# A spectral layer with two MLPs: x on all partitions, first transforms in four array tiles

## The chip, the cores and the metric

The kernel runs on one core of a Trainium2 chip. The metric is the time of one execution in device microseconds (us). The kernel before took 1102.35 us, the median of three runs (1100.9 to 1102.99).

## The reference, cut to what matters

```python
X = np.fft.rfft(x, axis=1)               # x: 2 x 3008 x 256, float32
Yr = Xr @ w_r - Xi @ w_i + b_r
Yi = Xr @ w_i + Xi @ w_r + b_i
Y = soft_threshold(Yr, 0.01) + 1j * soft_threshold(Yi, 0.01)
y = np.fft.irfft(Y, n=3008, axis=1)
h = y.reshape(6016, 256) @ w_in;   g = max(h, 0) + alpha * min(h, 0);    z = g @ w_out     # 2048 wide
h = z @ w_in2;   g = where(h >= 1, h, where(h <= -1, 0, (h + 1)**2 / 4));   out = g @ w_out2
```

All is computed in float32; products of the MLPs and of the mixing are made in three parts each from a high and a low half.

## The kernel before, in words

The transform of length 3008 is split as 47 x 64. A first transform of length 47 is a matmul with a constant (`c47`), for 24 frequencies k, cosine and sine. Its result `a` goes to memory (`a_dr`) and comes back with the 64 other positions in the partitions. A second transform per k (`psf`, from `a` and the constants `m`), the mixing with the weights (`psk`, `ri`), the threshold and the first half of the way back (`psi`, constants `n`) follow; its result `ve` goes through memory (`v_dr`) too, and `p3` (line 613) ends the way back. Then the two MLPs run.

x comes in 16 groups (two batches b, eight each; the host pads 47 rows to 48), each [96 partitions, 4, 256], 384 KB: two parities of position times 48 rows. `f1(g)` makes the first transform of group g in two PSUM banks, each with two matmuls of 256 columns (line 397); a float32 matmul appears in the profile as two records. ScalarE evicts one bank (line 399), VectorE the other (line 401), to `ae`. `store_a(g, h)` (line 375) writes half h of `ae` (48 partitions, 12 frequencies, 192 KB) to `a_dr[b][h]`, in pieces of 1 KB. `load_a(b, parts)` (line 371) reads some k of `a` back into `a_sb[b]`, [128 partitions, 24, 256].

Every engine works in the order in which the program is written; a planner sets nothing. SyncE (SP) issues nearly all transfers, in order, and waits before an issue whose inputs aren't ready; what stands behind waits too. Its order before is: the first eight groups of x; for each of the groups 0 to 7 its first store and the load of group g + 8; `load_a(0)` of k 0 to 3, then of 4 to 11, with constants between; the eight second stores of batch 0; constants; `load_a(0)` of k 12 to 23; constants; the first weights (line 147); the first stores of batch 1 and later, in the item loop, its second stores. ScalarE's queue issues `c47`, `alpha`, the bias and the two weight matrices `wm32`.

TensorE does the 16 first transforms, then 24 items (b, i), two k each, 12 a batch. In the loop over j, `psf` of item j + 2 (line 448, eight records) comes first, then `psk` of item j + 1, `ri` of item j and `psi` of item j - 2. At j = 2 and from j = 5 on, steps of the generator `conversions` are taken: they load MLP weights and split them on ScalarE, VectorE and GpSimd (POOL). The loads of `a` of batch 1 are issued at j = 5, 6 and 9.

Of the kernel before, what the change touches and what calls it, by code (L numbers as in the profile page):

```python
# [25 lines left out]
W_MAX = 122876.0 * 2.0 ** -16  # L26
NP = 6
CHUNKS = [512, 512, 512, 512, 512, 448]
PAIRS = [(0, 512), (1024, 512), (2048, 480)]


def fourier_constants():

    import numpy as np

    n1, k1 = np.arange(R1), np.arange(NK)
    a = 2 * np.pi * (np.outer(n1, k1) % R1) / R1

    c = np.zeros((2, 48, 2, 2, NK))
    for par in range(2):  # L40
        c[par, :R1, 0, par] = np.cos(a)
        c[par, :R1, 1, par] = -np.sin(a)
    c = c.reshape(96, 4, 2, NK // 2).transpose(0, 2, 1, 3).reshape(96, 96)

    g = np.zeros((2, 64, 64))
    g[:, 0:96 // 2:2, :R1] = np.cos(a).T
    g[:, 1:96 // 2:2, :R1] = -np.sin(a).T
    g = g.reshape(128, 64)

    t, par, k2 = np.arange(NT), np.arange(2), np.arange(R2)  # L50
    n2 = t[:, None] + 32 * par[None, :]
    m = np.zeros((NT, 2, 2, NK, 2, R2))
    w = np.zeros((2, R2, NK, 2, 2, NT))
    for k in range(NK):
        freq = k + R1 * k2
# [39 lines left out]
def spectral_mlp_kernel(ctx: ExitStack, tc: tile.TileContext, x, w_r, w_i, bias, c_f1, c_f2,  # L95
                        c_i1, c_i2, w_in1, w_out1, alpha, w_in2, w_out2, out):
    nc = tc.nc
    V, A, G, T = nc.vector, nc.scalar, nc.gpsimd, nc.tensor
# [3 lines left out]
    psum = ctx.enter_context(tc.tile_pool(name="psum", bufs=2, space=PSUM))  # L102
    dram = ctx.enter_context(tc.tile_pool(name="dram", bufs=1, space=DRAM))

    def split(src, hi, lo, hi_engine):

        if hi_engine is A:
            A.activation(hi, src, AF.Copy)  # L108
        else:
            V.tensor_copy(hi, src)  # L110
        V.tensor_tensor(lo, src, hi.bitcast(F32), op=ALU.subtract)  # L111
# [10 lines left out]
    def block(tag, shape, dtype, name):  # L122
        return base.tile(shape, dtype, tag=tag, name=name)
# [6 lines left out]
        p = block(f"p{npiece[0] % NP}", [128, 1024], F32R, name)  # L130
        return p[:, 112:112 + 768]

    a_dr = [[dram.tile([NT, 48, D], F32, name=f"a_dr{b}_{h}") for h in range(2)] for b in range(B)]
    v_dr = [dram.tile([96, NT, D], F32, name=f"v_dr{b}") for b in range(B)]


# [199 lines left out]
    def obank(shape, name, ahead=None):  # L336
# [2 lines left out]
        turn[0] += ahead is None  # L339
        return psum.tile(shape, F32, tag=f"o{k}", bufs=1, name=name)  # L340

    warm = rot.tile([128, 512], F32, tag="ta", name="warm")
    V.memset(warm, 0.0)
    ri = [psum.tile([128, 2, D], F32, tag=f"o{k}", bufs=1, name=f"ri{k}") for k in range(2)]
    for k in range(2):
        T.matmul(ri[k].rearrange("p z e -> p (z e)"), warm[:, 0:128], warm, start=True, stop=True)


    c47 = block("u2", [128, 1024], F32, "c47")[0:96, 0:96]
    A.dma_start(c47, c_f1)  # L350
    xs = {}

    def load_x(g):
        b, j = divmod(g, 8)
        tag = f"p{g}" if g < 6 else f"w{g - 6}" if g < 14 else f"c{g - 12}"
        xs[g] = block(tag, [96, 4, D], F32, f"x{b}_{j}")
        if g == 0:
            nc.sync.dma_start(xs[g][:, 0:1, :], x[b, j, :, 0:1, :])
            nc.sync.dma_start(xs[g][:, 1:4, :], x[b, j, :, 1:4, :])
        else:  # L360
            nc.sync.dma_start(xs[g], x[b, j])

    A_PARTS = ((0, 2), (2, 2), (4, 2), (6, 2), (8, 4), (12, 6), (18, 6))

    def load_a(b, parts):
        if a_sb[b] is None:
            a_sb[b] = block(f"a{b}", [128, NK, D], F32, f"a_{b}")
        for k, n in parts:
            h, k0 = divmod(k, NK // 2)
            src = a_dr[b][h].rearrange("t (q k) f -> (t q) k f", q=4)  # L370
            nc.sync.dma_start(a_sb[b][:, k:k + n, :], src[:, k0:k0 + n, :])

    def store_a(g, h):
        b, j = divmod(g, 8)
        nc.sync.dma_start(a_dr[b][h][4 * j:4 * j + 4].rearrange("t p f -> p t f"), aes[g][48 * h:48 * h + 48])

    def load_mn(k, tiles, src, h=None):

        s = slice(0, 8) if h is None else slice(4 * h, 4 * h + 4)
        nc.sync.dma_start(tiles[k][:, s, :].rearrange("p k f -> p (k f)"),  # L380
                          src[:, 1024 * k + 128 * s.start:1024 * k + 128 * s.stop])
# [2 lines left out]

    def f1(g):
        b, j = divmod(g, 8)
        if g < 10:
            ae = block(f"w{8 + g}" if g < 5 else f"m{1 + g}" if g < 8 else f"w{g - 8}", [96, 4, D], F32, f"ae{g}")
        else:
            if g == 10:  # L390
                late.append(block("a1", [96, 6, 4, D], F32, "ae_late"))
            ae = late[0][:, g - 10]
        aes[g] = ae
        for i in range(2):
            ps = psum.tile([96, 2, D], F32, tag="h" if i else "e", name=f"ps1_{b}_{j}_{i}")
            for u in range(2):
                T.matmul(ps[:, u, :], c47, xs[g][:, 2 * i + u, :], start=True, stop=True)
            if i == 0:
                A.activation(ae[:, 0:2, :], ps, AF.Copy)
            else:  # L400
                V.tensor_copy(ae[:, 2:4, :], ps)

    late = []
    for g in range(8):
        load_x(g)
# [9 lines left out]
    A.dma_start(b_t[0:1], bias)  # L415
    ones = rot.tile([1, 128], F32, tag="cm", name="ones")
    V.memset(ones, 1.0)
    for g in range(8):
        f1(g)
        store_a(g, 0)  # L420
        load_x(8 + g)
        if g == 3:
            load_mn(0, m_t, c_f2, 0)
        if g in (1, 2):
            A.dma_start(wm32[g - 1], (w_r, w_i)[g - 1].rearrange("(c p) e -> p c e", p=128))
    load_a(0, A_PARTS[:2])
    load_mn(0, m_t, c_f2, 1)
    load_a(0, A_PARTS[2:5])
    load_mn(1, m_t, c_f2, 0)
    load_mn(0, n_t, c_i1, 0)  # L430
    for g in range(8):
        store_a(g, 1)
    load_mn(1, m_t, c_f2, 1)
    load_mn(0, n_t, c_i1, 1)
    load_a(0, A_PARTS[5:])
    load_mn(1, n_t, c_i1)
    load_mn(2, m_t, c_f2)
    conv = conversions(0, list(range(NF)))
    next(conv)
    items = [(b, i) for b in range(B) for i in range(NK // 2)]  # L440
    xt, y_32, ve = {}, {}, {}

# [46 lines left out]
    wm = [block(t, [128, 2, 2, D], F32R, f"wm{k}") for k, t in enumerate(("c0", "c1", "w2"))]  # L489
    ws = [rot.tile([128, 2, D], F32, tag=t, name=f"ws{t}") for t in ("cm", "cp")]  # L490

    def split_wm(k, w):
        hi, lo = (wm[k][:, z].rearrange("p c (h q) -> p c q h", h=2) for z in range(2))
        split(w.rearrange("p c (q h) -> p c q h", h=2), hi, lo, A)

    for g in range(8, 16):
        f1(g)
        if g < 15:
            store_a(g, 0)
        if g == 8:  # L500
            T.matmul(ri[0].rearrange("p z e -> p (z e)"), ones, b_t[0:1].rearrange("p z e -> p (z e)"), start=True, stop=True)
            V.tensor_copy(b_t, ri[0])
        if g == 9:
            split_wm(0, wm32[0])
            V.scalar_tensor_tensor(ws[0], wm32[0], -1.0, wm32[1], op0=ALU.mult, op1=ALU.subtract)
        if g == 11:
            split_wm(1, ws[0])
            V.tensor_tensor(ws[1], wm32[1], wm32[0], op=ALU.subtract)
        if g == 13:
# [150 lines left out]
    n = len(items)  # L660
# [19 lines left out]
            ops[int(what[0])](what[1])  # L680
    for name in "HshLl":
        ops[2](name)
    store_a(15, 0)
    for j in range(n):
        parts = f2_parts(*items[j + 2]) if 0 < j < n - 2 else None
        if j + 1 < n:
# [4 lines left out]
        if j >= 2:  # L691
            i1(*items[j - 2])

        if j == 3:
            for g in range(8, 16):
                store_a(g, 1)
        if j == 5:
            load_a(1, A_PARTS[:2])
        if j == 6:
            load_mn(2, n_t, c_i1, 0)  # L700
            load_a(1, A_PARTS[2:3])
            load_mn(2, n_t, c_i1, 1)
            load_a(1, A_PARTS[3:5])
# [384 lines left out]
```

## Time and profile before

| what | value |
|---|---|
| median of three runs | 1102.35 us |
| profiled execution, its own time | 1102.65 us |
| its span | 1100.6 us |
| TensorE busy | 1087.2 us |
| VectorE busy | 897.4 us |
| ScalarE busy | 815.9 us |
| GpSimd busy | 36.9 us |
| moved by DMA | 101.19 MB |

The span runs from the first to the last instruction; the execution's own time has 2.05 us around it. A busy TensorE is not TensorE at its peak, since matmuls are pipelined and their ends are modelled: where it matters, starts are counted. L397 is line 397 of the kernel; PE is TensorE, PEld its weight loads, DVE VectorE, ACT ScalarE, POOL GpSimd, SP SyncE; a q behind the engine means its queue, which waits and issues transfers.

### The profile page before, as it was taken

Reading aid. Unit: us, or ns where it says so; the run is one execution under the profiler, and the core shown is the slowest. Engines: PE = TensorE matmul, PEld = TensorE weight load, DVE = VectorE, ACT = ScalarE, POOL = GpSimd, SP = SyncE. Lnnn points to the kernel's source line nnn. Section 1 sums busy time; section 2 is a strip of 40 time slices with the busy share of each in tenths; the row PEclk is TensorE's granted clock in tenths of the full one; section 3 lists DMA queues with packets and bytes.
Section 4 is the critical chain, followed back from the end, with each engine's and each line's share of the span. In section 5 each row is a group of like instructions: output and inputs, shape, how many; then the busy total and the mean of one; then the engine's idle time right before and its main releaser. Section 6 shows DMA issues by size and latency. Waiting matters only on the chain.

```text
span 1100.6 us, 17043 instructions
## 1 busy us (share of the span) xinstructions
PE 1087.2 (99%) x6368; PEld 955.7 (87%) x6368; DVE 897.4 (82%) x1572; ACT 815.9 (74%) x1499; POOL 36.9 (3%) x36
## 2 busy tenths in 40 slices
PE   9989999999999999999999999999999999999998
PEld 6878888888888998888889988888899888888897
DVE  3769759888879979989999877877878878878876
ACT  3557776656776768888888777877778878777876
POOL 0025400000000000000000000000000000000000
PEclk9999999999999999999999999999999999999999
DMA  9898754101322403324226720010010000100101
GB/s 265 299 277 261 204 142 108 39 1 67 126 97 97 171 20 115 115 96 141 89 97 248 273 90 1 1 39 1 1 38 1 37 1 1 39 1 1 39 1 37
DMA packets 49860, 101.19 MB, mean 92 GB/s; under 512 B 5009, under 2 KB 27249, under 8 KB 49778
## 3 DMA queue, kind: packets, MB, share of 16 engines
q1 hardware_dynamic: 48832, 99.41, 27.6%
q8 instruction: 50, 0.82, 0.3%
q10 hardware_dynamic: 946, 0.69, 0.2%
q14 instruction: 32, 0.26, 0.1%
HBM read 64.57 MB, written 35.52 MB: 91 GB/s over the span
## 4 chain that ended last, share of the span: by engine, by line
PE 82%; ACT 3%; DVE 2%; issue 0%; ACTq 0%; DVEq 0%
PE pq L114 10%; PE pq L115 10%; PE pq L116 10%; PE seeded L114 4%; PE seeded L116 4%; PE seeded L115 4%; PE psh L114 4%; PE pso L114 4%; PE psh L116 4%; PE psh L115 4%; PE pso L116 4%; PE pso L115 4%; PE psA L114 3%; PE psA L116 3%; PE psA L115 3%; PE psC L116 3%
## 5 line engine op out<-in xcount | busy, mean ns | idle before, releaser
L114 PE MATMUL pq<-gh,w 128*128 128x512 f32 (+1 forms) x576 | 216.6, 376 | 1.0 <-ACT yt L874 1.0
L115 PE MATMUL pq<-gl,w 128*128 128x512 f32 (+1 forms) x576 | 216.0, 375 | 0.4 <-DVE gl L845 0.2
L116 PE MATMUL pq<-gh,w 128*128 128x512 f32 (+1 forms) x576 | 215.8, 375 | 0.0
L842 ACT ACTIVATE gh<-ta 128x512 fp32r<-128x512 f32 (+1 forms) x144 | 88.0, 619 | 92.1 <-DVE ta L839 85.9
L641 ACT ACTIVATE ta<-psh,slopes 128x512 f32<-128x512 f32 (+1 forms) x96 | 65.1, 678 | 78.7 <-DVE ta L643 42.3
L114 PEld LDWEIGHTS pq<-gh,w 128*128 128x128 f32 x576 | 108.8, 189 | 15.9 <-ACT yt L874 3.1
L115 PEld LDWEIGHTS pq<-gl,w 128*128 128x128 f32 x576 | 108.9, 189 | 13.7 <-DVE gl L845 1.0
L116 PEld LDWEIGHTS pq<-gh,w 128*128 128x128 f32 x576 | 108.9, 189 | 12.8
L845 DVE TENSOR_TENSOR gl<-tb,gh 128x512 fp32r<-128x512 f32 (+1 forms) x96 | 65.3, 680 | 60.8 <-ACT gh L842 60.7
L845 DVE TENSOR_TENSOR gl<-ta,gh 128x512 fp32r<-128x512 f32 (+1 forms) x144 | 97.3, 676 | 3.1 <-ACT gh L842 1.4
L111 DVE TENSOR_TENSOR gl<-ta,gh 128x512 fp32r<-128x512 f32 (+1 forms) x96 | 65.2, 679 | 37.9 <-ACT gh L108 37.5
L933 DVE TENSOR_TENSOR h<-psC,s 128x512 f32<-128x512 f32 (+1 forms) x72 | 48.8, 678 | 40.8 <-PE psC L116 34.1
L114 PE MATMUL psh<-mxh,w 128*128 128x512 f32 (+1 forms) x192 | 72.2, 376 | 0.1
L114 PE MATMUL pso<-gh,w 128*128 128x512 f32 (+1 forms) x192 | 72.3, 377 | 0.0
L116 PE MATMUL pso<-gh,w 128*128 128x512 f32 (+1 forms) x192 | 71.9, 375 | 0.0
L115 PE MATMUL psh<-mxl,w 128*128 128x512 f32 (+1 forms) x192 | 71.9, 375 | 0.0
L116 PE MATMUL psh<-mxh,w 128*128 128x512 f32 (+1 forms) x192 | 71.9, 375 | 0.0
L115 PE MATMUL pso<-gl,w 128*128 128x512 f32 (+1 forms) x192 | 71.9, 375 | 0.0
L643 DVE SCALAR_TENSOR_TENSOR ta<-psh,slopes,ta 128x512 f32<-128x512 f32 (+1 forms) x96 | 70.5, 734 | 0.0
L839 DVE SCALAR_TENSOR_TENSOR tb<-tb,h 128x512 f32<-128x512 f32 (+1 forms) x96 | 60.7, 673 | 0.0
L831 ACT ACTIVATE ta<-ta 128x512 f32<-128x512 f32 (+1 forms) x96 | 59.3, 617 | 1.6
L842 ACT ACTIVATE gh<-tb 128x512 fp32r<-128x512 f32 (+1 forms) x96 | 59.3, 618 | 0.0
(163 smaller groups left out, 2640.1 us busy)
## 6 DMA issues: line engine op xcount, KB each, us to landing
s<-kept SPq DMA_DIRECT2D x32, 512.0 KB, 4.3
u<-in_w_in SPq DMA_DIRECT2D x32, 256.0 KB, 3.0
u<-in_w_out SPq DMA_DIRECT2D x32, 256.0 KB, 3.3
kept<-sh SPq DMA_DIRECT2D x16, 512.0 KB, 2.9
kept<-wh SPq DMA_DIRECT2D x16, 512.0 KB, 2.7
w<-kept SPq DMA_DIRECT2D x16, 512.0 KB, 5.5
v_dr<-ve SPq DMA_DIRECT2D x12, 512.0 KB, 3.9
v<-v_dr SPq DMA_DIRECT2D x32, 192.0 KB, 5.3
```

Of the source, the lines that this page charges most:

```text
L111: V.tensor_tensor(lo, src, hi.bitcast(F32), op=ALU.subtract)
L114: T.matmul(ps, wl, xh, start=start, stop=False, skip_group_check=chained)
L115: T.matmul(ps, wh, xl, start=False, stop=False, skip_group_check=chained)
L116: T.matmul(ps, wh, xh, start=False, stop=stop, skip_group_check=chained)
L641: A.activation(ta, ps, AF.Copy, scale=slope[:, f:f + 1])
L643: V.scalar_tensor_tensor(ta, ps, sign[:, f:f + 1], ta, op0=ALU.mult, op1=ALU.max)
L831: A.activation(self.t, self.t, AF.Square)
L839: V.scalar_tensor_tensor(self.t, self.t, 1.0, self.h, op0=ALU.min, op1=ALU.max)
L842: A.activation(halves(self.gh, self.m), like_halves(self.t, self.m), AF.Copy)
L845: V.tensor_tensor(halves(self.gl, self.m), like_halves(self.t, self.m), halves(self.gh, self.m).bitcast(F32), op=ALU.subtract)
L933: V.tensor_tensor(blk.h, ps[x], ps[y_], op=ALU.add)
```

## The change

The host lays x out so that one group's 96 rows come in two transfers: 64 rows to every second partition from 0, 32 rows to every fourth from 1. The groups come in 11 chunks of one or two, 22 transfers, all issued at once by SP. Each group of x has its own buffer: six in the space of `a` of batch 0, six in that of batch 1, four in pieces. As 32 partitions of a group are not written by the transfers, every buffer is first set to zero, by VectorE (half of group 0; 3, 6, 9) and GpSimd (the rest).

`c47` has 128 partitions and 64 columns. `f1(g)` makes four matmuls of 64 rows, 64 columns out and 512 columns through: two parities in the rows, and the two halves q of the group's four positions in the columns. `ae` has 128 partitions. Of each 64 rows, every fourth holds k 0 to 7, every second one k 8 to 23 and the rest nothing.

The first store of batch 0 takes k 0 to 7 (32 partitions, 128 KB), the second k 8 to 23 (64 partitions, 256 KB); batch 1 has one store of all 128 partitions (512 KB). ScalarE's queue issues the first stores of groups 0 to 3, SP those of 4 to 7. `load_a` now makes two transfers, one for each half of 64 partitions. The stores of batch 1 are written in the loop of the groups 8 to 15, and `load_a(0, 12, 12)`, with constants and the first weights, behind that loop. The weight matrices' loads move to SP, two weight sums to GpSimd, and the bias's matmul to group 5.

```diff
+X_CHUNKS = [(0, 1), (1, 1), (2, 2), (4, 2), (6, 2), (8, 2), (10, 2), (12, 1), (13, 1), (14, 1), (15, 1)]
...
-    a_dr = [[dram.tile([NT, 48, D], F32, name=f"a_dr{b}_{h}") for h in range(2)] for b in range(B)]
+    a_dr = [dram.tile([8, 4, 2, k, D], F32, name=f"a_dr{k}") for k in (16, 32, 64)]
...
+    for tag, groups in (("a0", 6), ("a1", 6), ("p0", 1), ("p1", 1), ("p2", 1), ("p3", 1)):
+        t = block(tag, [128, groups, 4, D], F32, f"x_{tag}")
...
+    V.memset(xs[0][:, 0:2], 0.0)
+    G.memset(xs[0][:, 2:4], 0.0)
     warm = rot.tile([128, 512], F32, tag="ta", name="warm")
     V.memset(warm, 0.0)
+    for g in range(1, 16):
+        (V if g in (3, 6, 9) else G).memset(xs[g], 0.0)
...
+    def load_x(g, n):
+        o = 96 * 1024 * g
+        t = xs[g].rearrange("p (o t) f -> p o t f", o=1) if n == 1 else x_of[g // 6][:, g % 6:g % 6 + n]
+        for rows, step in ((64, 2), (32, 4)):
+            src = x[o:o + rows * n * 1024].rearrange("(p o t f) -> p o t f", p=rows, o=n, t=4)
+            nc.sync.dma_start(t[step // 4:128:step], src)
+            o += rows * n * 1024
+
+    def load_a(b, k, n):
...
+        h = k >= 8
+        if b:
+            src = a_dr[2].rearrange("j w q (z k s) f -> z s (j w q) k f", z=2, s=4 - 2 * h)[:, int(h)]
+        else:
+            src = a_dr[h].rearrange("j w q (z k) f -> z (j w q) k f", z=2)
+        for z in range(2):
+            nc.sync.dma_start(a_sb[b][64 * z:64 * z + 64, k:k + n, :], src[z][:, k - 8 * h:k - 8 * h + n])
+
+    def store_a(g, h=2, engine=None):
         b, j = divmod(g, 8)
-        nc.sync.dma_start(a_dr[b][h][4 * j:4 * j + 4].rearrange("t p f -> p t f"), aes[g][48 * h:48 * h + 48])
+        rows = slice(None) if b else slice(h, 128, 4 - 2 * h)
+        (engine or nc.sync).dma_start(a_dr[h][j].rearrange("w q i f -> (q i) w f"), aes[g][rows].rearrange("p s r f -> p (s r) f"))
...
-        for i in range(2):
-            ps = psum.tile([96, 2, D], F32, tag="h" if i else "e", name=f"ps1_{b}_{j}_{i}")
-            for u in range(2):
-                T.matmul(ps[:, u, :], c47, xs[g][:, 2 * i + u, :], start=True, stop=True)
-            if i == 0:
-                A.activation(ae[:, 0:2, :], ps, AF.Copy)
-            else:
-                V.tensor_copy(ae[:, 2:4, :], ps)
+        ps = [psum.tile([128, 2, D], F32, tag="eh"[r], name=f"ps1_{b}_{j}_{r}") for r in range(2)]
+        for q in range(2):
+            for r in range(2):
+                rows = slice(64 * r, 64 * r + 64)
+                T.matmul(ps[r][64 * q:64 * q + 64], c47[rows, :], xs[g][rows, q:4:2, :], start=True, stop=True)
+        A.activation(ae[:, :, 0], ps[0], AF.Copy)
+        V.tensor_copy(ae[:, :, 1], ps[1])
...
+    for k, (g, size) in enumerate(X_CHUNKS):
+        load_x(g, size)
+        if k in (4, 5):
+            nc.sync.dma_start(wm32[k - 4], (w_r, w_i)[k - 4].rearrange("(c p) e -> p c e", p=128))
     for g in range(8):
         f1(g)
+        if 1 <= g <= 4:
+            store_a(g - 1, 0, A)
...
+    for g in range(4, 8):
         store_a(g, 0)
...
+    load_mn(0, m_t, c_f2)
+    load_a(0, 0, 2)
+    load_a(0, 2, 6)
     for g in range(8):
         store_a(g, 1)
...
+    load_mn(0, n_t, c_i1)
+    load_mn(1, m_t, c_f2)
+    load_a(0, 8, 4)
...
     for g in range(8, 16):
         f1(g)
-        if g < 15:
-            store_a(g, 0)
+        store_a(g)
...
+    load_a(0, 12, 12)
+    load_mn(1, n_t, c_i1)
+    load_mn(2, m_t, c_f2)
+    next(conv)
```

## Rows read from the trace of the kernel before

**Rows 1.** The page: busy us by engine; DMA busy tenths in 40 slices.
```profile
PE 1087.2 (99%) x6368; PEld 955.7 (87%) x6368; DVE 897.4 (82%) x1572; ACT 815.9 (74%) x1499; POOL 36.9 (3%) x36
...
DMA  9898754101322403324226720010010000100101
```

**Rows 2.** TensorE's groups by shape, 0 to 36 us: count, busy us, mean ns, idle before.
```profile
L397 PE MATMUL ps<-x,c 96*96 96x256 f32 x128 | 28.9, 386 | 0.3 <-DMA x<-in_x 0.3
```

**Rows 3.** The timeline, TensorE: start us, duration us, line, tiles, records, releaser.
```profile
1.45 3.78 PE L346 MATMUL ri<-warm 128*128 128x512 f32 x4 [1.45 <-DVE warm L343]
5.03 1.40 PE L397 MATMUL ps<-x,c 96*96 96x256 f32 x3
...
9.71 11.60 PE L397 MATMUL ps<-x,c 96*96 96x256 f32 x53
```

**Rows 4.** Windows: stretch, length, busy by engine (instructions), granted clock, DMA share, GB/s.
```profile
6.00:14.00 8.00, 8.00 (x38) 6.03 (x37) 2.75 (x4) 2.79 (x5) 0.00 (x0) 1.00 1.03 261
42.00:44.00 2.00, 2.00 (x21) 2.00 (x20) 1.97 (x6) 1.53 (x4) 0.00 (x0) 1.00 1.09 383
50.00:54.00 4.00, 4.00 (x35) 3.50 (x34) 2.65 (x5) 2.31 (x7) 0.00 (x0) 1.00 0.99 406
...
60.00:64.00 4.00, 4.00 (x35) 3.50 (x34) 2.94 (x8) 3.10 (x8) 0.62 (x1) 1.00 0.78 166
...
104.00:108.00 4.00, 4.00 (x35) 3.50 (x35) 3.92 (x9) 2.79 (x8) 1.88 (x2) 1.00 0.99 216
```

**Rows 5.** The timeline, psf of items 0, 1, 4, 6, 9 and 12.
```profile
35.19 1.16 PE L448 MATMUL psf<-m,a 128*128 128x128 f32 x8
36.54 1.13 PE L448 MATMUL psf<-m,a 128*128 128x128 f32 x8 [0.19 <-DMA a<-a_dr]
...
44.99 1.06 PE L448 MATMUL psf<-m,a 128*128 128x128 f32 x8
...
53.41 1.16 PE L448 MATMUL psf<-m,a 128*128 128x128 f32 x8
...
65.90 1.16 PE L448 MATMUL psf<-m,a 128*128 128x128 f32 x8
...
82.61 1.13 PE L448 MATMUL psf<-m,a 128*128 128x128 f32 x8 [1.73 <-ACT fh L471]
```

**Rows 6.** The timeline, TensorE: one p3 group in 64x64 tiles and what follows it.
```profile
111.71 1.15 PE L613 MATMUL ps<-slopes,v 48*64 48x47 f32 x64
112.79 1.16 PE L448 MATMUL psf<-m,a 128*128 128x128 f32 x8
```

**Rows 7.** Groups by shape of ScalarE, VectorE (0 to 36 us) and POOL (all).
```profile
L399 ACT ACTIVATE ae<-ps 96x512 f32<-96x512 f32 x10 | 5.9, 593 | 14.6 <-PE ps L397 14.6
...
L401 DVE COPY ae<-ps 96x512 f32<-96x512 f32 x10 | 6.9, 687 | 15.5 <-PE ps L397 14.3 <-DMA x<-in_x 1.2
...
L343 DVE MEMSET warm<- 128x512 f32 x1 | 0.5, 485 | 0.9 <-PEq L1076 0.9
...
L193 POOL TENSOR_SCALAR cm<-cm 128x512 f32<-128x512 f32 x8 | 6.1, 768 | 62.8 <-DMA a_dr<-ae_late 62.8
```

**Rows 8.** The timeline: issues of transfers by SP, start and duration in us.
```profile
0.74 0.39 SPq L358 DMA_DIRECT2D x<-in_x  x1
...
31.98 2.02 SPq L371 DMA_DIRECT2D a<-a_dr  x2
...
47.73 0.80 SPq L371 DMA_DIRECT2D a<-a_dr  x2
...
50.98 0.89 SPq L375 DMA_DIRECT2D a_dr<-ae  x2
...
102.92 2.67 SPq L598 DMA_DIRECT2D v<-v_dr  x6
```

**Rows 9.** ScalarE's waits, 60 to 90 us: who for what, us in total, times, longest.
```profile
ACT ve L548 <- DMA v_dr<-ve: 3.3, 1, 3.3
...
ACT cm L163 <- DMA u<-in_w_out: 2.8, 2, 2.6
```

More of the change, by code (lines that the diff above doesn't have):

```diff
@@ L37, in fourier_constants @@
     a = 2 * np.pi * (np.outer(n1, k1) % R1) / R1
[L39 to L43, printed above, removed]
+    cs = np.stack([np.cos(a), -np.sin(a)], axis=1)
+    c = np.zeros((2, 64, 64))
+    rows = np.array([2 * i if i < 32 else 4 * (i - 32) + 1 for i in range(R1)])
+    c[:, rows[:, None], 4 * np.arange(16)] = cs[:, :, :8].reshape(R1, 16)
+    c[:, rows[:, None], 2 * np.arange(32) + 1] = cs[:, :, 8:].reshape(R1, 32)
+    c = c.reshape(128, 64)
     g = np.zeros((2, 64, 64))
@@ L69, in fourier_constants @@
         w[0, :, k, 1], w[1, :, k, 1] = sw, cw * cj
+    m = m.reshape(8, 2, 2, 2, 2, NK, 2, R2).transpose(3, 0, 1, 4, 2, 5, 6, 7)
     w = w.reshape(2, R2, NK // 2, 2, 128).transpose(3, 1, 2, 0, 4)
@@ L340, in obank @@
         return psum.tile(shape, F32, tag=f"o{k}", bufs=1, name=name)
+    c47 = block("u2", [128, 1024], F32, "c47")[:, 0:64]
+    A.dma_start(c47, c_f1)
+    xs = []
+    for tag, groups in (("a0", 6), ("a1", 6), ("p0", 1), ("p1", 1), ("p2", 1), ("p3", 1)):
+        t = block(tag, [128, groups, 4, D], F32, f"x_{tag}")
+        xs += [t[:, g] for g in range(groups)]
+        if tag[0] == "a":
+            x_of = [t] if tag == "a0" else x_of + [t]
+    V.memset(xs[0][:, 0:2], 0.0)
+    G.memset(xs[0][:, 2:4], 0.0)
     warm = rot.tile([128, 512], F32, tag="ta", name="warm")
     V.memset(warm, 0.0)
+    for g in range(1, 16):
+        (V if g in (3, 6, 9) else G).memset(xs[g], 0.0)
     ri = [psum.tile([128, 2, D], F32, tag=f"o{k}", bufs=1, name=f"ri{k}") for k in range(2)]
@@ L346, in spectral_mlp_kernel @@
         T.matmul(ri[k].rearrange("p z e -> p (z e)"), warm[:, 0:128], warm, start=True, stop=True)
[L349 to L359, printed above, removed]
-        else:
-            nc.sync.dma_start(xs[g], x[b, j])
-    A_PARTS = ((0, 2), (2, 2), (4, 2), (6, 2), (8, 4), (12, 6), (18, 6))
-    def load_a(b, parts):
+    def load_x(g, n):
[6 more added lines that the diff above has]
+    def load_a(b, k, n):
         if a_sb[b] is None:
             a_sb[b] = block(f"a{b}", [128, NK, D], F32, f"a_{b}")
[L368 to L373, printed above, removed]
+        h = k >= 8
[6 more added lines that the diff above has]
+    def store_a(g, h=2, engine=None):
         b, j = divmod(g, 8)
-        nc.sync.dma_start(a_dr[b][h][4 * j:4 * j + 4].rearrange("t p f -> p t f"), aes[g][48 * h:48 * h + 48])
+        rows = slice(None) if b else slice(h, 128, 4 - 2 * h)
+        (engine or nc.sync).dma_start(a_dr[h][j].rearrange("w q i f -> (q i) w f"), aes[g][rows].rearrange("p s r f -> p (s r) f"))
     def load_mn(k, tiles, src, h=None):
@@ L386, in f1 @@
         b, j = divmod(g, 8)
[L387 to L393, printed above, removed]
-        for i in range(2):
-            ps = psum.tile([96, 2, D], F32, tag="h" if i else "e", name=f"ps1_{b}_{j}_{i}")
-            for u in range(2):
-                T.matmul(ps[:, u, :], c47, xs[g][:, 2 * i + u, :], start=True, stop=True)
-            if i == 0:
-                A.activation(ae[:, 0:2, :], ps, AF.Copy)
-            else:
-                V.tensor_copy(ae[:, 2:4, :], ps)
-    late = []
-    for g in range(8):
-        load_x(g)
+        tag = f"w{8 + g}" if g < 5 else f"m{1 + g}" if g < 8 else ("w0", "w1", "w3", "w4", "w5", "w6", "w7", "c3")[g - 8]
+        ae = aes[g] = block(tag, [128, 2, 2, D], F32, f"ae{g}")
+        ps = [psum.tile([128, 2, D], F32, tag="eh"[r], name=f"ps1_{b}_{j}_{r}") for r in range(2)]
[5 more added lines that the diff above has]
+        V.tensor_copy(ae[:, :, 1], ps[1])
     m_t = [block(f"m{k}", [128, 8, 128], F32, f"m{k}") for k in range(3)]
@@ L417, in spectral_mlp_kernel @@
     V.memset(ones, 1.0)
+    for k, (g, size) in enumerate(X_CHUNKS):
+        load_x(g, size)
+        if k in (4, 5):
+            nc.sync.dma_start(wm32[k - 4], (w_r, w_i)[k - 4].rearrange("(c p) e -> p c e", p=128))
     for g in range(8):
         f1(g)
-        store_a(g, 0)
[L421 to L430, printed above, removed]
+        if 1 <= g <= 4:
+            store_a(g - 1, 0, A)
+        if g == 5:
+            T.matmul(ri[0].rearrange("p z e -> p (z e)"), ones, b_t[0:1].rearrange("p z e -> p (z e)"), start=True, stop=True)
+            V.tensor_copy(b_t, ri[0])
+    for g in range(4, 8):
+        store_a(g, 0)
+    load_mn(0, m_t, c_f2)
+    load_a(0, 0, 2)
+    load_a(0, 2, 6)
     for g in range(8):
         store_a(g, 1)
[L433 to L437, printed above, removed]
+    load_mn(0, n_t, c_i1)
+    load_mn(1, m_t, c_f2)
+    load_a(0, 8, 4)
     conv = conversions(0, list(range(NF)))
-    next(conv)
     items = [(b, i) for b in range(B) for i in range(NK // 2)]
@@ L490, in spectral_mlp_kernel, with split_wm @@
     ws = [rot.tile([128, 2, D], F32, tag=t, name=f"ws{t}") for t in ("cm", "cp")]
-    def split_wm(k, w):
+    def split_wm(k, w, sign=1.0):
         hi, lo = (wm[k][:, z].rearrange("p c (h q) -> p c q h", h=2) for z in range(2))
-        split(w.rearrange("p c (q h) -> p c q h", h=2), hi, lo, A)
+        w = w.rearrange("p c (q h) -> p c q h", h=2)
+        A.activation(hi, w, AF.Copy, scale=sign)
+        if sign > 0:
+            V.tensor_tensor(lo, w, hi.bitcast(F32), op=ALU.subtract)
+        else:
+            for c in range(2):
+                V.scalar_tensor_tensor(lo[:, c], w[:, c], sign, hi[:, c].bitcast(F32), op0=ALU.mult, op1=ALU.subtract)
     for g in range(8, 16):
         f1(g)
-        if g < 15:
-            store_a(g, 0)
-        if g == 8:
-            T.matmul(ri[0].rearrange("p z e -> p (z e)"), ones, b_t[0:1].rearrange("p z e -> p (z e)"), start=True, stop=True)
-            V.tensor_copy(b_t, ri[0])
+        store_a(g)
         if g == 9:
             split_wm(0, wm32[0])
[L505 to L509, printed above, removed]
+            G.tensor_tensor(ws[0], wm32[1], wm32[0], op=ALU.add)
+        if g == 10:
+            G.tensor_tensor(ws[1], wm32[1], wm32[0], op=ALU.subtract)
+        if g == 12:
+            split_wm(1, ws[0], -1.0)
+        if g == 14:
             split_wm(2, ws[1])
+    load_a(0, 12, 12)
+    load_mn(1, n_t, c_i1)
+    load_mn(2, m_t, c_f2)
+    next(conv)
     def mix_sum(b, i, later=False):
@@ L682, in spectral_mlp_kernel @@
         ops[2](name)
-    store_a(15, 0)
     for j in range(n):
@@ L692, in spectral_mlp_kernel @@
             i1(*items[j - 2])
-        if j == 3:
-            for g in range(8, 16):
-                store_a(g, 1)
         if j == 5:
-            load_a(1, A_PARTS[:2])
+            load_a(1, 0, 4)
+            load_a(1, 4, 4)
         if j == 6:
[L700 to L703, printed above, removed]
+            load_mn(2, n_t, c_i1)
+            load_a(1, 8, 8)
         if j == 9:
-            load_a(1, A_PARTS[5:])
+            load_a(1, 16, 8)
             nc.sync.dma_start(g47, c_i2)
@@ L1066 @@
     xp[:, :, :, :R1] = x.reshape(B, R1, 2, NT // 4, 4, D).transpose(0, 3, 2, 1, 4, 5)
+    xp = [xp[:, :, :, k].reshape(16, -1, 1024).transpose(1, 0, 2) for k in (slice(0, 32), slice(32, 48))]
+    xp = np.concatenate([v[:, g:g + n].ravel() for g, n in X_CHUNKS for v in xp])
     c_f1, c_f2, c_i1, c_i2 = fourier_constants()
     arrays = {
-        "x": xp.reshape(B, NT // 4, 96, 4, D), "w_r": w_r, "w_i": w_i, "bias": np.stack([b_r, b_i])[None],
+        "x": xp, "w_r": w_r, "w_i": w_i, "bias": np.stack([b_r, b_i])[None],
         "c_f1": c_f1, "c_f2": c_f2, "c_i1": c_i1, "c_i2": c_i2,
```

## The prediction

> **What bounds the kernel now.** The page comes first: TensorE is busy 1087.2 of the span's 1100.6 us, while the row of DMA slices shows full engines in the first slices alone [rows 1]. The change touches only the first 150 us, so the rest is read there. The groups of TensorE by shape say that 128 matmul records of 96x256 make the first transforms [rows 2], and the timeline has them back to back, 53 in 11.60 us, 0.216 us each less the last one's tail [rows 3]. That stretch is TensorE's own: the only wait for x in it is 0.3 us [rows 2]. The windows show the second limit beside it: the DMA engines' share is 1.03 while x comes in, 1.09 while stores go out [rows 4]. The starts of psf, one per pair of frequencies (an item: 24, numbered from 0), give the pace afterwards [rows 5]: item 0 at 35.19, item 4 at 44.99, item 6 at 53.41, item 9 at 65.90: 4.16 us an item, without a wait. Item 12 comes at 82.61, 29.20 after item 6, where six times 4.16 are 24.96: 4.25 us go in gaps between items 9 and 12. TensorE takes all of the 4.16 us, so an item that starts late delays the kernel's end by as much, less what later gaps give back.
>
> **The first transforms.** Before: 16 groups of 8 records of 0.216 us, 1.73 us a group, 27.6 us. After: four tiles of 64x64 with 512 columns, two records each. Where the trace has four such tiles, 64 records with 47 columns start within 1.08 us (111.71 to the next group at 112.79), 17 ns each [rows 6]; a record of 256 columns takes 0.216, so one of 47 alone would take about 40 ns. The four do run side by side, and a group becomes two steps of 0.43 us: 0.86 us, 13.8 us in all. The evictions (593 and 687 ns a group [rows 7]) fit under it. So TensorE gives 13.8 us back here, if x and the DMA engines can use it. They can't: the rest is a sum of transfers, in the order of SP's queue.
>
> **Rates.** Four kinds stand in the windows [rows 4]. x to 96 partitions: 261 GB/s (6 to 14 us). Loads of a to 128 partitions: 406 (50 to 54). Stores in 1 KB pieces: 383 at a share of 1.09, so 350 a full engine set. Loads of v to 48 partitions of one half, then of the other: 216 (104 to 108, the six issued at 102.92 [rows 8]). The new x transfers (64 rows two apart, 32 rows four apart) occur nowhere; they reach all partitions as the 406 do, but each with few rows as the 261 do. The ends are 6.29 MB / 0.406 = 15.5 us and 6.29 / 0.261 = 24.1; I take the middle, 19.8. The loads of a now go in two halves of 64 partitions: that is nearest to v, 216; the other end is 406. The stores of b 0 take 32 or 64 strided partitions, of b 1 all 128: 350, with 213 as the other end (166 at a share of 0.78, 60 to 64 us, stores of partitions 0 to 47).
>
> The trace shows the halves of v at about half of the 406. The Trainium skill (SBUF — State Buffer, "Can I just issue two DMAs to hit both halves?") says the same of two transfers, one to each half: only 6% over one alone. It speaks against the new loads of a, and the 216 agrees.
>
> **The sum, in us from the span's start.**
> - The first x transfer waits for two memsets. DVE's of 512 columns took 0.485 [rows 7] and began at 0.91, so the issue moves from 0.74 to about 1.5, and first data to about 3.2. The other memsets are 12 on POOL; its nearest row, 128x512 with one input, took 768 ns [rows 7], so 1024 columns cost between 0 and 1.54 and the last ends at 0.45 + 0.77 + 12 x 1.54 = 19.7 at worst. They stay ahead of x, which is three quarters in by then. Were they late, SP would hold back everything behind them, stores and loads of a included.
> - x 19.8, the two weight matrices now on SP (0.52 MB at 350: 1.5) and ScalarE's four stores (0.52 MB: 1.5): the last x is in at 26.0. An issue costs about 0.4 [rows 8]; ScalarE's four, with an eviction of 0.59 each, fit under 1.2 us a group of x.
> - Four more first stores behind x: 1.5, to 27.5; the wait for their landing to 28.3. Before, the load of a issued at 31.98 let item 0 start at 35.19 [rows 5, 8], 3.2; half the rate adds 0.6. Item 0 at 32.1, 3.1 earlier than before.
> - k 2 to 7, 0.79 MB at 216: 3.6, item 1 at 35.7 (before, 1.35 after item 0). From item 1 to item 4 it was 8.45 us: item 4 would start at 44.2.
> - Meanwhile the queue holds eight second stores (2.10 MB, 6.0, to 41.7), two constants (1.05 MB at 406, 2.6, to 44.3) and k 8 to 11 (0.52 MB at 216, 2.4): 46.7. Item 4 at 46.7, and item 6 due 8.42 later [rows 5], at 55.1.
> - k 12 to 23 now stands behind all stores of b 1, eight of 512 KB: SP takes them in program order, where before these 12 frequencies were issued at 47.73 and b 1's first store at 50.98 [rows 8]. 4.19 MB at 350 is 12.0, to 58.7; then 1.57 MB at 216, 7.3: 66.0. Item 6 needs the whole transfer: it starts at 66.0, not 53.41, after 11 us of an idle TensorE.
> - From there the pace is 4.16. The two old gaps go: ScalarE waited 3.3 us there for a store of ve and 2.8 for a weight load [rows 9], both behind b 1's stores, which are now done by then. That gives 4.25 back.
> - After the idle time TensorE starts slowly: the four records of 512 columns at the very start took 5.03 - 1.45 = 3.58 us, where two of 256 columns later cost 0.43, so that 4 x 0.43 = 1.7 would do [rows 3]. About 1.8 us is lost once; the other end is 0.
> - Sum: 66.0 - 53.4 - 4.25 + 1.8 = +10. The weights' conversions and the v stores are tied to the items and move with them; the MLPs after 150 us are untouched. The profiled execution took 1102.65 us (0.3 above the median 1102.35), so 1112.
>
> What else moves costs nothing: the weight sums on POOL and the sign in DVE's split lie in the wait for a; the bias's matmul goes into the x stream. SP's wait for the second stores has eight stores of b 1 and k 12 to 23 behind it, but the two constants ahead of it fill the queue for 2.6 us.
>
> **Rivals.**
> - x at 406, because over two transfers every partition group gets equal shares: everything 4.3 earlier, item 6 at 61.7, +5.7: 1108. For it: loads over 128 partitions run so. Against: no transfer with fewer rows did. Chance 20%. The Trainium skill's port map (SBUF — State Buffer, "Door 1: The DMA port swizzle") puts 0 to 95 twice as heavily on one set of ports as on the other and the new rows evenly on all sixteen; by that rule this rival would be the case, and the 261 against 406 agrees.
> - x at 261 still, bound by how few rows each of 16 engines gets: 4.3 later, 1116. Chance 17%.
> - On the other side: the halves of a run beside each other at 406, and x does too. 3.15 MB before item 6 then cost 7.7 instead of 14.6, item 6 starts at about 54.9, hardly idle before it, and with the gaps gone it ends 1.5 - 4.25 = 2.8 us earlier: 1100. It decides from item 6 before 53.4 + 4.25 = 57.7. For it: 64 rows divide evenly where 48 don't. Against: the 216. Chance 18%.
> - The tiles don't run side by side with different moving rows (in [rows 6] they share them): 3.46 us a group, 55 in all, item 0 at 60, item 6 at 78, +22: 1125. Chance 4%.
> - The forecast: 41%, with 1107 to 1117 as its own range (stores at the slower rate, the gaps only partly gone, no slow restart).
>
> **How the numbers follow.** About 0.2% is what can be told from no change. Of the third rival's 18%, 12 are faster by more and 6 the same; the lower edge of the first (faster loads of a, or stores above 350) gives 2 of faster and 5 of the same. So faster 0.14, same 0.11, slower 0.75. The range leaves out the serial tiles and the far ends: 1099 to 1120.
>
> **What would show it.** Right: first-transform groups 0.9 us of TensorE each and waiting for x; DMA windows of x between 261 and 406; item 0 near 32; one wait of psf for a of about 11 us before item 6, near 66; no gaps between items 9 and 12; later stages equal. Wrong: loads of a in halves well over 216 GB/s; item 6 before 58; a wait of SP for POOL; records of 512 columns that follow one another singly.

## The result, and the profile after

The changed kernel takes 1113.61 us, the median of four runs (1111.68 to 1115.11); the kernel before, on the same chip, 1102.67. The ratio is 1.0097, with a 95% interval from 1.0072 to 1.0122: about 11 us slower. The profiled execution took 1113.03 us, its span is 1111.2, 10.6 more than the 1100.6 before.

The page: TensorE is busy for 5.2 us less than in [rows 1] though the span is longer, and the DMA row differs in its first slices above all.

```profile
span 1111.2 us, 17068 instructions
...
PE 1082.0 (97%) x6368; PEld 944.0 (85%) x6368; DVE 898.8 (81%) x1575; ACT 815.4 (73%) x1499; POOL 50.6 (5%) x51
...
DMA  8979746100233403223326740010010000100100
```

The timeline of TensorE, one run of first transforms and psf of items 0, 1, 4, 6, 7, 12 and 23 (start, duration, line, tiles, records, idle time before and its releaser):

```profile
10.55 3.86 PE L404 MATMUL ps<-x_a,c 64*64 64x512 f32 x32 [2.36 <-DMA x_a<-in_x]
...
33.39 2.05 PE L450 MATMUL psf<-m,a 128*128 128x128 f32 x8 [1.50 <-DMA a<-a_dr]
36.72 2.04 PE L450 MATMUL psf<-m,a 128*128 128x128 f32 x8 [1.28 <-DMA a<-a_dr]
...
46.66 1.13 PE L450 MATMUL psf<-m,a 128*128 128x128 f32 x8 [0.73 <-DMA a<-a_dr]
...
66.30 2.05 PE L450 MATMUL psf<-m,a 128*128 128x128 f32 x8 [11.27 <-DMA a<-a_dr]
72.58 1.16 PE L450 MATMUL psf<-m,a 128*128 128x128 f32 x8
...
93.39 1.16 PE L450 MATMUL psf<-m,a 128*128 128x128 f32 x8
...
144.57 1.16 PE L450 MATMUL psf<-m,a 128*128 128x128 f32 x8
```

Beside [rows 5]: item 0 is 1.8 us early, item 4 1.7 late, item 6 12.9 late, behind 11.27 us in which TensorE waits for a. Item 7 is 15.0 late (57.58 before), since TensorE restarts slowly. Items 7 to 12 follow at 4.16 each without a gap, where before 4.25 us went in gaps, so item 12 is 10.8 late; item 23, at 133.75 before, is 10.8 late too. From there to the end it is 966.6 us, against 966.9 before: the whole difference was made before item 12.

Windows of the changed kernel (stretch, length, busy by engine, then granted clock, DMA share, GB/s):

```profile
0.00:8.00 8.00, 5.79 (x20) 1.72 (x20) 4.53 (x7) 1.88 (x2) 7.47 (x13) 1.00 0.65 176
3.00:10.00 7.00, 4.98 (x20) 1.21 (x18) 3.35 (x6) 1.68 (x3) 7.00 (x9) 1.00 0.91 280
10.00:12.00 2.00, 1.45 (x16) 0.60 (x16) 0.28 (x1) 0.32 (x1) 1.93 (x3) 1.00 0.99 406
13.00:16.00 3.00, 3.00 (x25) 0.90 (x22) 2.16 (x4) 1.33 (x3) 0.00 (x0) 1.00 0.57 186
...
14.00:18.00 4.00, 3.34 (x22) 0.81 (x18) 2.97 (x5) 1.98 (x4) 0.00 (x0) 1.00 0.81 258
22.00:26.00 4.00, 3.75 (x26) 0.91 (x18) 2.10 (x4) 2.52 (x5) 0.99 (x1) 0.87 1.02 405
26.00:36.00 10.00, 7.45 (x39) 3.16 (x38) 5.46 (x10) 4.48 (x7) 0.00 (x0) 0.86 0.92 246
36.00:44.00 8.00, 7.28 (x51) 7.31 (x52) 5.43 (x12) 4.12 (x10) 0.00 (x0) 0.74 1.04 366
...
46.00:56.00 10.00, 8.37 (x68) 7.33 (x68) 7.07 (x14) 5.85 (x14) 0.00 (x0) 1.00 1.08 373
58.00:64.00 6.00, 0.00 (x0) 0.00 (x0) 0.00 (x0) 0.00 (x0) 0.00 (x0) 0.50 0.99 209
64.00:72.00 8.00, 5.70 (x30) 5.59 (x32) 1.95 (x4) 1.61 (x4) 0.00 (x0) 0.57 0.95 318
```

Against [rows 4]: x now reaches 406 GB/s (10 to 12, and 405 from 22 to 26 us), not 261, but 280 from 3 to 10 us and 186 from 13 to 16, where the engines are busy for 0.57 of the time; the stores of b 1 (46 to 56) at 373 with a share of 1.08; the loads of a in halves (58 to 64) at 209 with full engines, while every compute engine stands still.

The queue of SP (start and time of its issues), one row of ScalarE's queue among them, and the waits (who for what, us in total, times, longest):

```profile
1.49 8.24 SPq L369 DMA_DIRECT2D x_a<-in_x  x10
...
8.32 0.69 ACTq L386 DMA_DIRECT2D a_dr<-ae  x1
...
14.38 0.42 SPq L423 DMA_DIRECT2D wm<-in_w_r  x1
...
42.78 10.21 SPq L386 DMA_DIRECT2D a_dr<-ae  x8
53.05 2.75 SPq L381 DMA_DIRECT2D a<-a_dr  x2
```

```profile
SPq L423 <- DMA a_dr<-ae: 4.6, 1, 4.6
...
PE psf L450 <- DMA a<-a_dr: 14.8, 4, 11.3
PE ps L404 <- DMA x_a<-in_x: 4.7, 3, 2.4
```

The reader is to see the two places where the order of a queue decides. Eight stores of 512 KB are issued from 42.78 on and the load of k 12 to 23 only behind them, at 53.05; before, its issue stood at 47.73 ahead of the first of them [rows 8]. And SP issues nothing from 9.7 to 14.4: the load of a weight matrix, which needs nothing that anyone computes, waits 4.6 us for a store of ScalarE's queue, issued at 8.32.

### The profile page after: what moved, and what is told of

It is laid out like the page before. It is cut to its first block, busy times and chain, and to the rows that moved or that the text cites. A ratio compares the mean times of both kernels' runs of the same rounds, so it can differ in the third digit from the quotient of the medians.

```text
span 1111.2 us, 17068 instructions
## 1 busy us (share of the span) xinstructions
PE 1082.0 (97%) x6368; PEld 944.0 (85%) x6368; DVE 898.8 (81%) x1575; ACT 815.4 (73%) x1499; POOL 50.6 (5%) x51
## 4 chain that ended last, share of the span: by engine, by line
PE 81%; ACT 2%; DVE 1%; issue 0%; ACTq 0%; DVEq 0%
PE pq L117 10%; PE pq L118 10%; PE pq L119 10%; PE seeded L117 4%; PE seeded L119 4%; PE seeded L118 4%; PE psh L117 4%; PE pso L117 4%; PE psh L119 4%; PE psh L118 4%; PE pso L119 4%; PE pso L118 4%; PE psA L117 3%; PE psA L119 3%; PE psA L118 3%; PE psC L119 3%
```

## The experiments

Each variant was timed beside the kernel before: that took 1103.26 us for the first four and 1102.86 for the last three, 1102.67 for the changed kernel. Differences of under 1 us between variants therefore say nothing.

**k 12 to 23 ahead of the stores of b 1.** Only the order of the queue is changed.

```diff
     load_a(0, 8, 4)
+    load_a(0, 12, 12)
+    load_mn(1, n_t, c_i1)
+    load_mn(2, m_t, c_f2)
...
     for g in range(8, 16):
         f1(g)
-        store_a(g)
...
-    load_a(0, 12, 12)
-    load_mn(1, n_t, c_i1)
-    load_mn(2, m_t, c_f2)
+    for g in (15, *range(8, 15)):
+        store_a(g)
```

> Changed kernel, but k 12 to 23 and the two constants are issued ahead of batch 1's eight stores (and of those, group 15's first, since its buffer is wanted again first). Theory: item 6 waits for the transfers that stand ahead of k 12 to 23 in SP's order. Then these land 12 us of stores earlier, at about 54; item 6 is due at 50.8 + 4.2 = 55.0 and starts there, within 1 us, instead of at 66.3. Not all of the 11 us is kept: batch 1's stores now go out from 57 to 69, beside the items, as before the change, and the store of ve stands behind them, so gaps of up to 5 us in all come back between items 7 and 12. Time 1100 to 1105. Rival, that the DMA engines' load as a whole sets the time and not its order: item 6 at 55, but item 12 no earlier than 92, time 1110 to 1114. Rival, that TensorE's lowered clock in the first 45 us costs most: item 4 stays at 46.7 either way, and the time falls by less than 3 us.

1109.19 us (seven runs), ratio to before 1.0056 [1.0035, 1.0076]. The 11 us of waiting are gone, but only 4.4 us of time: the size was missed, and the time lies between the range of the theory and that of the first rival, whose mark, item 12 no earlier than 92, was missed too: it comes at 90.08. Its timeline (psf of items 4, 6 and 9) and ScalarE's wait between 58 and 92 us:

```profile
50.20 1.13 PE L453 MATMUL psf<-m,a 128*128 128x128 f32 x8 [2.28 <-DMA a<-a_dr]
...
58.50 1.16 PE L453 MATMUL psf<-m,a 128*128 128x128 f32 x8
...
75.31 2.05 PE L453 MATMUL psf<-m,a 128*128 128x128 f32 x8 [4.25 <-DVE fl L474]
```

```profile
ACT cm L166 <- DMA u<-in_w_out: 4.6, 1, 4.6
```

Item 6 comes 8.30 after item 4 and waits for nothing, 7.8 us earlier than in the changed kernel. It isn't 11.3 earlier, and not at the 55 that was expected, since item 4 itself comes 3.5 later (50.20 for 46.66), behind a load of a. But the stores of b 1 are now issued until 64.2, and the weights of the MLP behind them: ScalarE, in order, waits 4.6 us for one of them with psf's evictions queued behind it, and the gap of [rows 5, 9] is back, with a slow restart: items 8 to 10 take 14.93 us instead of 8.32. The order is worth 7.8 us at item 6, and the 2.1 of the changed kernel's slow restart behind it; of these 9.9 the gap takes 6.6 again, by what the stores now delay.

**Each load of a in one transfer of 128 partitions.** The rows of the constant m are put in another order on the host.

```diff
...
-            src = a_dr[h].rearrange("j w q (z k) f -> z (j w q) k f", z=2)
-        for z in range(2):
-            nc.sync.dma_start(a_sb[b][64 * z:64 * z + 64, k:k + n, :], src[z][:, k - 8 * h:k - 8 * h + n])
+            src = a_dr[h].rearrange("j w q (z k) f -> (j w q z) k f", z=2)
+        nc.sync.dma_start(a_sb[b][:, k:k + n, :], src[:, k - 8 * h:k - 8 * h + n])
```

> Changed kernel, but a comes back in one transfer over 128 partitions in place of two of 64 (the partitions of a reordered, the host's constant m with them). Theory: the halves run at about half rate (205 against 406 GB/s). Then k 0 to 7 cost 2.6 us less, k 8 to 11 1.3, k 12 to 23 3.8: item 0 at 32.7, item 4 at 43 to 44, item 6 at 58.5 to 59.5 instead of 66.3; time 1104 to 1106. Rival, that the rate is set by the small number of bytes in flight or by memory and not by the partitions: item 6 stays at 65 to 66.5, time within 1.5 us of 1113.

1111.24 us (four runs), ratio 1.0066 [1.0042, 1.009]. The last part of the load in two windows (it landed at 64.24; a constant of 128 partitions stands behind it), and psf of items 4 and 6 in the timeline:

```profile
62.00:64.00 2.00, 0.00 (x0) 0.00 (x0) 0.00 (x0) 0.00 (x0) 0.00 (x0) 0.50 0.96 397
62.00:66.00 4.00, 1.63 (x8) 1.66 (x8) 0.00 (x0) 0.00 (x0) 0.00 (x0) 0.50 0.98 400
```

```profile
49.12 1.13 PE L449 MATMUL psf<-m,a 128*128 128x128 f32 x8 [0.86 <-PE ri L487]
...
64.37 2.04 PE L449 MATMUL psf<-m,a 128*128 128x128 f32 x8 [6.89 <-DMA a<-a_dr]
```

The rate is 397 to 400 where the halves had 209, and the wait 4.4 us shorter: the rival is refuted. The time fell by 2.4 only and item 6 came at 64.37, not near 59, since item 4 was at 49.12, 2.5 later than in the changed kernel: the x phase, which this edit doesn't touch, ended later, with SP waiting 4.9 us for one store of ScalarE and again for another. Why it fell out worse there is open; one profile can't tell it from chance.

**All first stores issued by SP, behind x.** The rival here was that ScalarE's early stores save time.

```diff
     for g in range(8):
         f1(g)
-        if 1 <= g <= 4:
-            store_a(g - 1, 0, A)
...
-    for g in range(4, 8):
+    for g in range(8):
         store_a(g, 0)
```

> Changed kernel, but SP issues all eight first stores of batch 0, behind x, and ScalarE none. Theory: in the changed kernel SP stands still from 9.7 to 14.4 us because its load of a weight matrix waits until ScalarE's first store has landed (the eight completion semaphores go round over both queues), and the DMA engines run dry. Without ScalarE's stores x is in at 21 to 22 instead of 26.4, all later transfers come about 3.5 us earlier, item 0 at 30, item 6 at 62.5 to 63.5; time 1109 to 1111. Rival, that the stores issued early save as much as the wait costs: item 0 within 1 us of 33.4 and time within 1.5 us of 1113.

1113.78 us (four runs), ratio 1.009 [1.0066, 1.0114]: no change against 1113.61. Two windows of x, and psf of items 0 and 6:

```profile
10.00:18.00 8.00, 7.29 (x42) 2.28 (x46) 3.46 (x5) 2.39 (x4) 2.33 (x4) 0.79 1.02 411
13.00:16.00 3.00, 3.00 (x24) 0.75 (x16) 1.85 (x3) 1.53 (x3) 0.00 (x0) 0.83 1.02 407
```

```profile
33.01 1.13 PE L448 MATMUL psf<-m,a 128*128 128x128 f32 x8 [3.14 <-DMA a<-a_dr]
...
66.30 2.05 PE L448 MATMUL psf<-m,a 128*128 128x128 f32 x8 [11.79 <-DMA a<-a_dr]
```

SP's wait is gone, x runs through at 411 and is in at 23.2 instead of 26.4. But the four more stores then stand behind x, the last first store lands at 27.57 instead of 27.77, and item 0 moves by 0.4. The rival was right: the wait is real, and the early stores give back what it costs. Of the 3.1 us by which x is earlier, an estimated 1.3 belong to the four stores' own 0.52 MB (at 406 GB/s), which no longer lie among x; the rest is left for the wait, during which the changed kernel's engines ran at 0.57 from 13 to 16 us and here at 1.02.

**x in two halves of 48 rows** (partitions 0 to 47 and 64 to 111). The rows of `c47` and the host's layout of x follow; all else is as changed.

```diff
-        for rows, step in ((64, 2), (32, 4)):
-            src = x[o:o + rows * n * 1024].rearrange("(p o t f) -> p o t f", p=rows, o=n, t=4)
-            nc.sync.dma_start(t[step // 4:128:step], src)
+        for half in range(2):
+            src = x[o:o + 48 * n * 1024].rearrange("(p o t f) -> p o t f", p=48, o=n, t=4)
+            nc.sync.dma_start(t[64 * half:64 * half + 48], src)
```

> Changed kernel, but x goes to partitions 0 to 47 and 64 to 111 in two transfers of 48 rows, not to 64 and 32 rows strided over all partitions. Theory: the strided rows run at 406 GB/s because they reach all partitions evenly, and rows that fill one half at 205 to 216: x takes 30 us of transfers, not 15.5, some of it in the time in which SP stands still; last x at 36 to 40 instead of 26.4, item 0 at 43 to 47, item 6 at 76 to 80; time 1122 to 1128. Rival, that the rate of x comes from the larger pieces (8 KB) and the longer queue: x windows stay near 400 GB/s and the time within 2 us of 1113.

1129.81 us (four runs), ratio 1.0235 [1.021, 1.0261]. A window of x, and psf of items 0 and 6:

```profile
20.00:30.00 10.00, 6.66 (x28) 1.44 (x29) 2.12 (x4) 1.19 (x2) 0.00 (x0) 0.67 0.93 193
```

```profile
48.70 2.05 PE L450 MATMUL psf<-m,a 128*128 128x128 f32 x8 [4.99 <-DMA a<-a_dr]
...
83.01 2.05 PE L450 MATMUL psf<-m,a 128*128 128x128 f32 x8 [11.53 <-DMA a<-a_dr]
```

193 GB/s with the engines at 0.93: the same bytes occupy them twice as long. Item 0 is 15.3 us later, item 6 16.7, the end 16.2, each somewhat more than was expected. The pieces are as large as in the changed kernel, so the rival is refuted: where the rows lie is worth this much. The Trainium skill (SBUF — State Buffer, "Door 1: The DMA port swizzle") lets the rate depend on how many of 16 ports a transfer's partitions reach; two transfers of one half each at 193, and the strided ones over both halves at 406, agree. That count alone does not give the 261 GB/s of the kernel before [rows 4], whose rows 0 to 95 reach all 16 by the same map; there the measurement decides.

**Each first-transform matmul made twice**, so that TensorE needs 27 us for them again.

```diff
-        for q in range(2):
+        for q in (0, 1, 0, 1):
```

> Changed kernel, but every first-transform matmul runs twice into the same place: the 16 groups cost TensorE 2 x 13.8 = 27.6 us, as much as before the change. Theory: the 13.8 us that the four tiles save are not on the path, since x and then the transfers ahead of k 12 to 23 set the time. Then item 0 comes at 34 to 36 (the last groups end at about 35), item 4 within 1 us of 46.7, item 6 at 66 to 67, time within 2 us of 1113.6. Rival, that the tiles carry what gain there is: items 0 and 6 come 8 to 14 us later, time 1121 to 1127. Second rival, that TensorE's granted clock, at 0.5 from 33 to 40 us, costs more than the work: with TensorE busy through the x stream it stays at 1.0, items 0 to 4 take 10 instead of 13.3 us, and still item 6 at 66.

1115.29 us (four runs), ratio 1.0111 [1.0093, 1.0129], 1.7 above the changed kernel. Two windows, and psf of items 0, 4 and 6:

```profile
26.00:36.00 10.00, 10.00 (x96) 5.06 (x88) 5.74 (x9) 6.26 (x9) 0.00 (x0) 1.00 0.82 252
36.00:44.00 8.00, 6.36 (x51) 5.73 (x49) 6.00 (x12) 4.37 (x11) 0.00 (x0) 1.00 1.04 345
```

```profile
36.15 1.16 PE L450 MATMUL psf<-m,a 128*128 128x128 f32 x8
...
50.25 1.53 PE L450 MATMUL psf<-m,a 128*128 128x128 f32 x8 [3.15 <-DMA a<-a_dr]
...
68.91 2.04 PE L450 MATMUL psf<-m,a 128*128 128x128 f32 x8 [8.66 <-DMA a<-a_dr]
```

TensorE has 14 us more to do and the end moves by 1.7 (3.3 between the two profiled executions): the four tiles are nearly worthless here, since x and the transfers behind it set the pace. Item 0 no longer waits for a, but for the first transforms; item 6 for a, as before. Items 4 and 6 missed their expectation by 2.6 and 1.9 us: SP's load of the second weight matrix waited 6.3 us for a store of ScalarE, and SP issued k 8 to 11 at 44.18, not at 41.56. Of the second rival, the clock did stay at 1.00, but items 0 to 4 took 14.1 us all the same.

**Order and whole loads together.** The edits of the first two experiments.

> The orders of the early kernel (k 12 to 23 and two constants ahead of batch 1's stores, group 15's first) and the single transfers of a over 128 partitions together; the rest as changed. Theory: both act on the same wait, so the gains don't add up. Item 6 is due without a wait (item 4 at 46 to 50, item 6 8.3 later, 54 to 58); batch 1's stores go out beside the items, 2 to 3 us earlier than in the early kernel, so the gaps between items 8 and 11 shrink from 6.5 to 2 to 4 us. Time 1103 to 1107. Rival, that gaps come from the engines that convert the weights and not from transfers: they stay at 6.5 and the time at 1107 to 1110.

1104.46 us (ten runs), ratio 1.0019 [1.0006, 1.0032]. Psf of items 6 and 9:

```profile
55.44 1.16 PE L452 MATMUL psf<-m,a 128*128 128x128 f32 x8
...
70.94 1.13 PE L452 MATMUL psf<-m,a 128*128 128x128 f32 x8 [2.94 <-DVE fl L473]
```

Two edits give back 9.2 of the 10.9 us, more than the 4.4 and 2.4 of each alone, where the expectation had them overlap: with the order alone, item 4 was at 50.20, behind loads in halves; here it is at 47.09. The gap ahead of item 9 is 2.94, and ScalarE's wait for the MLP weights 3.2.

**The whole queue in the order of need.** Whole loads; k 12 to 23 and constants early; all first stores by SP, with x of groups 12 to 15 behind them; half of b 1's stores behind the first MLP weights, in the item loop.

```diff
-    for k, (g, size) in enumerate(X_CHUNKS):
+    for k, (g, size) in enumerate(X_CHUNKS[:7]):
         load_x(g, size)
...
+    for g in range(8):
         store_a(g, 0)
+    for g, size in X_CHUNKS[7:]:
+        load_x(g, size)
...
+    for g in (15, 8, 9, 10):
+        store_a(g)
     next(conv)
...
+        if j == 3:
+            for g in range(11, 15):
+                store_a(g)
```

> All transfers in the order in which they are wanted: x of groups 0 to 11, batch 0's first stores (all by SP), x of 12 to 15, the constants, a of k 0 to 7, second stores, constants, k 8 to 11, k 12 to 23, constants, four of batch 1's stores (group 15's first), the first weights; the other four stores at j = 3, behind the store of ve; a in one transfer over 128 partitions. Theory: what the strided x and the tiles save is then kept: x is in at 22 to 24, item 0 at 26 to 29 instead of 33.4, item 6 at 47 to 50 without a wait, gaps under 3 us later; time 1093 to 1098, 5 to 10 us under the kernel before. Rival, that the gaps of the items (ScalarE, VectorE, the lowered clock) take it back: item 6 as early, but item 12 no more than 2 us earlier than before (82.6), time 1100 to 1104.

1098.81 us (12 runs), ratio 0.9963 [0.9952, 0.9975]: 0.4% faster than the kernel before, 4.1 us below its 1102.86 and about 15 below the changed one. Psf of items 0 and 1 in one row, then of items 4, 6 and 12; a window of x of groups 12 to 15; and ScalarE's wait:

```profile
34.38 3.97 PE L452 MATMUL psf<-m,a 128*128 128x128 f32 x16 [2.54 <-DMA a<-a_dr]
...
46.76 1.13 PE L452 MATMUL psf<-m,a 128*128 128x128 f32 x8 [1.12 <-issue]
...
55.05 1.16 PE L452 MATMUL psf<-m,a 128*128 128x128 f32 x8
...
80.03 1.16 PE L452 MATMUL psf<-m,a 128*128 128x128 f32 x8
```

```profile
24.00:30.00 6.00, 4.74 (x24) 0.81 (x24) 2.31 (x5) 2.25 (x4) 0.00 (x0) 0.72 0.84 264
```

```profile
ACT cm L166 <- DMA u<-in_w_out: 0.6, 1, 0.6
```

From item 4 on there is no gap, and item 12 is 2.6 us ahead of [rows 5]. Item 0 missed its expectation, 34.38 for 26 to 29: eight small transfers of x, issued about 0.7 us apart, ran at 264 GB/s, and the first load of a, issued behind them at 26.95, landed at 34.24. Item 6 is late by as much, 55.05 for 47 to 50, and the time just outside its range. What order would bring item 0 forward was not tried, and how much of the gain is the order's and how much the whole loads' was not taken apart.

## Why the prediction was right

The forecast was +10 and 1112; measured are +10.6 of span and 1113.61. Its steps in turn:

- **Tiles.** Forecast 0.86 us a group: four groups took 3.86, 0.97 each with the last one's tail, and TensorE's waits for x come to 4.7 us. Right, and the doubled matmuls show that the gain is lost behind x.
- **x.** The last x was forecast in at 26.0, and landed at 26.37. The sum was right and its composition wrong. The rate that x reaches is that of the first rival, 406 and not the middle value. Two stretches filled most of the 4.3 us between these two rates. From 3 to 10 us the engines moved 280 GB/s: against 406 that is 0.88 MB less, an estimated 2.2 us, and why x starts so slowly is open. From 13 to 16 us they moved 186, an estimated 1.6 us less, behind a wait that the forecast didn't have: SP stood 4.6 us for a store of ScalarE, and in the third experiment, without it, this stretch ran at 407. That the errors met is luck.
- **First stores, item 0, item 1.** Landed at 27.8, forecast 28.3; item 0 at 33.4 for 32.1, item 1 at 36.7 for 35.7. The load of a was issued at 27.96 and its second half landed at 33.26: 5.3 us with a constant of 512 KB ahead in the queue, which the sum had left out, where 3.8 had been allowed.
- **Item 4.** 46.66 for 46.7, held by the load of k 8 to 11 as forecast (0.73 us of waiting). The clock fell beside it, which the forecast didn't have: TensorE's granted clock was 0.86 between 26 and 36 us and 0.74 to 44, 0.5 in parts of it, the lower level of 1.2 GHz, after stretches in which it waited for x and a. With the matmuls doubled TensorE was busy for all of 16 to 36 us, and the clock stayed at 1.00 until 44; item 4 waited for a there too, 3.15 us. So the load sets item 4; what the lower clock costs by itself no run shows.
- **Item 6.** 66.30 for 66.0. b 1's stores: forecast done at 58.7 at 350 GB/s for full engines, landed at about 58.5, 373 at 1.08, or 345. k 12 to 23 then 7.3 us at 216, landed at 66.17, at 209. The idle time of 11 us came as 11.27. The first two experiments show that both terms are real: the order, and the rate of the halves. Here the Trainium skill's rule that two transfers, one to each half, gain only 6% over one alone (SBUF — State Buffer, "Can I just issue two DMAs to hit both halves?") agrees; 209 against 400 is shown.
- **The gaps.** 4.25 us were to come back; there is no gap between items 9 and 12. They return, 4.25 and 2.94, as soon as b 1's stores stand behind k 12 to 23: their cause, the MLP weights queued behind these stores, was read rightly: with four of the eight stores behind the weights, in the last experiment, ScalarE's wait is 0.6 and there is no gap.
- **The slow restart.** 1.8 forecast, 2.1 measured: item 7 follows item 6 after 6.28 us instead of 4.16, at a granted clock of 0.57, after the wait at 0.50.
- **Memsets and later stages.** GpSimd's 12 took 0.95 us each, within 0 to 1.54; SP waited 0.7 us for them, which the forecast had called a mark of its being wrong; it is too little to move a term of the sum. After item 23 nothing moved.

Of the rivals, x at 406 came true as a rate and not as a time; x at 261 and the tiles one after the other are refuted; the halves side by side at 406 is refuted by 209.

## What to carry to other kernels

Where one queue issues nearly everything, write down the order of need beside the order of issue: here a load needed by item 6 stood behind 4.19 MB that item 12 was the first to need, and TensorE waited 11.3 us for it, where a faster transform and a faster x together had brought item 0 forward by 1.8. Before making an engine faster, ask what it waits for afterwards; 14 us of TensorE were worth 2 to 3. And moving a wait is not removing it: each reordering brought the next transfer late, until the whole queue was in order.

## What was not expected of the hardware

- **A queue can wait for the other queue's transfer.** In the trace the transfers of SP and ScalarE count up the same eight semaphores in turn; a later issue waits until the last transfer on its semaphore has landed. The wait stands in the issuing instruction itself, so it is the program's. So SP's load of a weight matrix, with no input to wait for, stood 4.6 us (11.0 with x in halves) behind a 128 KB store which ScalarE had issued in the middle of the x stream and which took 6.0 us to land.
- **Rows two and four apart can run at the full rate.** 64 and 32 rows a transfer reached 406 GB/s, like the 128-partition loads; rows side by side in one half at about 200 with the engines busy.
- **GpSimd's memset** of 128x1024 took 953 ns, VectorE's 912.
